# Values of two groups of four heads in one TensorE stretch, a re-planned order, stores held back by a microsecond, and x's low parts on GpSimd

## The chip, the cores and the metric

The kernel runs on one core of a Trainium2 chip. The metric is device time in microseconds (us) of one execution. Three executions of the kernel before took 1021.41, 1022.13 and 1023.31 us; the median is 1022.13.

## The reference

One transformer block on x of 2048 tokens by 640, in fp32: sliding-window attention with 32 heads of 20 (each query sees itself and the 255 keys before it), then a gated feed-forward layer of width 1536, each behind a layer norm and with a residual.

```python
def _A_ref(x, wqkv, wo):
    B, S, D = x.shape
    H = 32; Dh = D // H; W = 256
    qkv = (lambda x, *d: x.transpose(*d))((x @ wqkv).reshape(B, S, 3, H, Dh), 2, 0, 3, 1, 4)
    q, k, v = qkv[0], qkv[1], qkv[2]
    scores = jnp.einsum("bhqd,bhkd->bhqk", q, k) * (Dh ** -0.5)
    idx = jnp.arange(S)
    mask = (idx[:, None] - idx[None, :] >= 0) & (idx[:, None] - idx[None, :] < W)
    scores = jnp.where(mask[None, None], scores, -1e9)
    p = _softmax(scores, axis=-1)
    o = jnp.einsum("bhqk,bhkd->bhqd", p, v)
    return (lambda x, *d: x.transpose(*d))(o, 0, 2, 1, 3).reshape(B, S, D) @ wo

def _B_ref(x, w_gate, w_up, w_down):
    return (_gelu(x @ w_gate) * (x @ w_up)) @ w_down

h = x + _A_ref(_layernorm(x, axis=-1), A_wqkv, A_wo)
h2 = h + _B_ref(_layernorm(h, axis=-1), B_w_gate, B_w_up, B_w_down)
```

## The kernel before

The 2048 tokens are 16 blocks of 128. The dense products (q, k and v, the output projection, the feed-forward layer) split each fp32 operand into a high and a low fp16 part and add three fp16 products. The low part is the operand minus its high part; for x and h of blocks behind the fourth this is done in `turned`: ScalarE writes the high half, VectorE the low half, and two DMA transposes on SP's queue bring both into place (tiles xp, xh, xl).

Attention works block by block in three steps, each on another shape of TensorE's array.

- `maxima` multiplies queries with the keys of the window in tiles of 64 by 64 (rows `ra<-kT,qT` and `rb<-kT,qT`), two heads by two halves of the queries at once. `max_out` lets VectorE add a mask (`mask` for the first two blocks, `band` behind them) and take the row's maximum in one instruction, into `b.mx`; the masked scores themselves go to a bf16 tile `junk` that nobody reads. The maxima are turned and become two extra rows of q.
- `scores` multiplies again, keys as weights, with those extra rows, so that the maximum is subtracted already (`ra<-qT,kT`, `rb<-qT,kT`). `score_out` lets ScalarE take the exponential into an SBUF tile `pt`, and GpSimd clear what lies outside the window with affine selects. A `pt` tile holds four heads (two pairs) and there are three of them; the selects run once for all four heads, when both pairs are there: two of 128x256 and one of 128x512 for a full window.
- `value_lane` multiplies the four heads' `pt` with v, in four column strips of 21 beside each other, fp32 (`pv<-pt,v`). A column of ones in v yields the sum. One stretch is one group of four heads, so a block has eight of them. After every fourth group ScalarE copies the PSUM bank `pv` (oT), and TensorE turns it, VectorE divides, and the result is split for the output projection.

Maxima and scores use the PSUM banks `ra` and `rb` (two banks each), dense products `mm` (two), the values `pv` and transposes `tp`. Between the attention pieces TensorE does dense products: q and k of later chunks of two blocks (weights w0, w1), v (w2), the output projection (w3), and, late, the first feed-forward products. After attention the feed-forward layer runs alone on TensorE.

The order is no list in the source: a planner (`Clock`, `Engine`, and `Lane.start` with the loop behind it) issues the instructions in the order in which it expects them to become ready. `Engine.cost` holds an expected duration for each instruction, `Clock.issue` keeps each engine's expected time, and a lane's next step is issued when the engines that it names are expected to be free soon and its operands to be ready (`self.need() <= now + 0.1`). The steps that only issue a transfer on SP name `("sync",)` alone. SP and ScalarE issue transfers from their queues. While nothing can be issued and no score has been, the planner puts a filler on TensorE: an identity times itself into `pv` (`pv<-ident`).

Rows of the profile carry line 199, the helper through which the planner records every instruction, so tile names tell the steps apart. `PE` rows of fp32 products show two records for one instruction.

## Time and profile before

| | |
|---|---|
| median of three runs | 1022.13 us |
| profiled execution, its own time | 1023.17 us |
| its span, first to last instruction | 1021.3 us |
| TensorE busy | 999.8 us (98%) |
| VectorE busy | 754.8 us (74%) |
| ScalarE busy | 437.0 us (43%) |
| GpSimd busy | 298.0 us (29%) |
| mean granted TensorE clock | 1.00 |

The first values start at 92 us and the last at 574; before lie loads, layer norms and the first projections, behind it the feed-forward layer alone. A group's row reads: line, engine, operation, out<-in by tile names, partitions x elements and type, count, then busy us and mean ns of one, then idle time of the engine just ahead and what ended most of it. A timeline row reads: start, length in us, engine, line, operation, count. PE is TensorE's matmul row, PEld its weight loads, DVE is VectorE, ACT ScalarE, POOL GpSimd, SP SyncE.

### The profile page before, as it was taken

How to read it: one execution, taken by the hardware profiler on the slowest of the kernel's cores; microseconds unless marked ns; L12 is line 12 of the kernel's file. 1: busy time of each engine (PE TensorE's matmuls, PEld its weight loads, DVE VectorE, ACT ScalarE, POOL GpSimd, SP SyncE). 2: the span in 40 equal slices, each digit the busy share in tenths (PEclk: the TensorE clock that was granted, in tenths of full speed). 3: DMA queues.
4: the chain of work that ended last, by engine and by line, in shares of the span. 5: the costliest groups of instructions: out<-in, count | busy, mean ns of one | idle time of the engine just before them, and what ended most of it. 6: DMA issues, size and time to landing. Idle time of an engine off the chain costs nothing.

```text
span 1021.3 us, 30777 instructions
## 1 busy us (share of the span) xinstructions
PE 999.8 (98%) x12921; PEld 695.8 (68%) x12921; DVE 754.8 (74%) x2221; ACT 437.0 (43%) x706; POOL 298.0 (29%) x489
## 2 busy tenths in 40 slices
PE   8999999999999999999999999999999999999998
PEld 7875666676666676776655564567777777777776
DVE  6888998986787787474788788798996975544553
ACT  6514654656555564654558543522222222221220
POOL 7102223443343342342436321255313310000000
PEclk9999999999999999999999999999999999999999
DMA  8657667361551524225033433223553532222211
GB/s 306 137 116 175 184 145 168 81 163 55 91 122 44 114 57 118 42 61 127 3 131 106 92 117 103 78 104 127 161 177 90 161 138 78 78 96 86 78 53 52
DMA packets 105835, 112.67 MB, mean 110 GB/s; under 512 B 38369, under 2 KB 79585, under 8 KB 105697
## 3 DMA queue, kind: packets, MB, share of 16 engines
q1 hardware_dynamic: 93600, 99.97, 35.9%
q10 hardware_dynamic: 12096, 10.75, 3.4%
q8 instruction: 101, 1.65, 0.7%
q14 instruction: 38, 0.30, 0.1%
HBM read 73.73 MB, written 28.84 MB: 100 GB/s over the span
## 4 chain that ended last, share of the span: by engine, by line
PE 82%; DVE 8%; DMA 4%; ACT 2%; issue 2%; SPq 1%; POOL 0%; ACTq 0%; DVEq 0%
PE mm L199 41%; PE pv L199 12%; PE ra L199 11%; PE rb L199 10%; PE tp L199 7%; DVE junk L199 2%; DVE am L199 1%; DVE ht L199 1%; DMA v<-in_wqkv_dram 1%; DMA gu<-in_wqkv_dram 1%; SPq L199 1%; DMA qT<-mT 1%; DVE m L199 1%; ACT pt L199 1%; DMA h_dram<-ht 1%
## 5 line engine op out<-in xcount | busy, mean ns | idle before, releaser
L199 POOL TENSOR_SCALAR_AFFINE_SELECT pt<-pt 128x512 f32<-128x512 f32 x352 | 175.3, 513 | 278.2 <-ACT pt L199 262.6
L199 DVE CUSTOM_DVE_ANT_0 junk<-rb,band 128x320 bf16<-128x320 f32 x230 | 112.5, 489 | 41.3 <-PE rb L199 35.9
L199 DVE CUSTOM_DVE_ANT_0 junk<-ra,band 128x320 bf16<-128x320 f32 x218 | 106.6, 489 | 43.8 <-PE ra L199 38.3
L199 ACT ACTIVATE pt<-ra,esc 128x640 f32<-128x640 f32 (+2 forms) x131 | 99.6, 767 | 66.2 <-PE ra L199 53.3
L199 ACT ACTIVATE pt<-rb,esc 128x640 f32<-128x640 f32 (+2 forms) x125 | 94.9, 766 | 77.2 <-PE rb L199 56.5
L199 PE MATMUL pv<-pt,v 128*21 128x128 f32 x2880 | 104.1, 275 | 1.1 <-ACT oT L199 1.1
L199 PEld LDWEIGHTS <-ah 128*128 128x128 f16 x768 | 75.0, 98 | 29.5 <-issue 2.1
L199 ACT ACTIVATE gel<-gel,ffk 128x512 f32<-128x512 f32 x36 | 26.0, 721 | 138.0 <-DVE gel L199 138.0
L199 PEld LDWEIGHTS pv<-pt,v 128*21 128x21 f32 x2880 | 68.6, 100 | 11.9 <-issue 2.1
L199 PEld LDWEIGHTS <-ws 128*128 128x128 f16 x720 | 70.3, 98 | 8.3
L199 PEld LDWEIGHTS <-kT 62*64 62x64 f16 x2880 | 61.9, 107 | 13.9 <-issue 10.1
L199 PEld LDWEIGHTS <-qT 60*64 60x64 f16 x1280 | 29.8, 104 | 60.3 <-issue 51.3
L199 PEld LDWEIGHTS <-gu 128*128 128x128 f16 x440 | 42.1, 98 | 36.1 <-issue 2.5
L199 DVE SCALAR_TENSOR_TENSOR ht<-mm,ffk,ht 128x320 f32<-128x320 f32 x96 | 52.1, 545 | 10.9 <-PE mm L199 9.0
L199 ACT CAST ah<-gel 128x512 f16<-128x512 f32 x48 | 29.6, 617 | 64.4 <-DVE gel L199 64.2
L199 PE MATMUL mm<-xh,w1h 128*128 128x256 f16 x200 | 54.7, 274 | 1.3 <-DVE qks L199 1.3
L199 PE MATMUL mm<-xl,w1h 128*128 128x256 f16 x200 | 54.7, 273 | 0.0
L199 PE MATMUL mm<-xh,w1l 128*128 128x256 f16 x200 | 54.7, 273 | 0.0
L199 PE MATMUL mm<-w3l,oh 128*128 128x320 f16 x160 | 48.1, 301 | 0.1
L199 PE MATMUL mm<-w2h,xh 128*128 128x320 f16 x160 | 48.1, 300 | 0.0
L199 PE MATMUL mm<-w2h,xl 128*128 128x320 f16 x160 | 48.1, 301 | 0.0
L199 PE MATMUL mm<-w3h,ol 128*128 128x320 f16 x160 | 48.1, 300 | 0.0
(299 smaller groups left out, 2521.3 us busy)
## 6 DMA issues: line engine op xcount, KB each, us to landing
ws<-wsums SPq DMA_DIRECT2D x24, 640.0 KB
qk<-qks ACTq DMA_DIRECT2D x32, 256.0 KB
qT<-qk SPq DMA_DIRECT2D x48, 160.0 KB
kT<-qk SPq DMA_DIRECT2D x48, 160.0 KB
wsums<-ws SPq DMA_DIRECT2D x12, 640.0 KB
ht<-in_x_dram SPq DMA_DIRECT2D x16, 320.0 KB
h_dram<-ht SPq DMA_DIRECT2D x16, 320.0 KB
ht<-h_dram SPq DMA_DIRECT2D x16, 320.0 KB
```

Of the source, the lines that this page charges most:

```text
L199: r = real(*args, **kw)
```

## The change

1. *Values of two groups together.* `pt` tiles now hold one pair of heads, and there are seven (RP) in place of three of two pairs. GpSimd's selects run per pair, at half the width. `value_lane` waits until two groups are ready and multiplies both in one stretch.
2. *VectorE's reduce writes in place.* `junk` goes; the masked scores overwrite their input in PSUM. `mask` and `band` become bf16, and an unused tile of ones goes.
3. *x's low parts by GpSimd.* In `turned`, for x (not for h), the subtraction moves from VectorE to GpSimd.
4. *Expected durations.* `Engine.cost` changes for several operations, and so the order of the whole program does.
5. *Transfers held.* A step that only issues a transfer on SP (but `stack` and `load_lane`) is issued when its operands are expected to have been ready for 1 us (HELD), where before it could be up to 0.1 us ahead of them.

```diff
-            switch, k.mode = SWITCH * (k.mode != mode), mode
+            switch = (SWITCH + 0.02 * (k.mode == "col")) * (k.mode != mode)
+            k.mode = mode
...
             if beside:
-                return 0.004
+                return 0.0005
...
-            return 0.065 + 0.00106 * m + 0.06 * (op == "scalar_tensor_tensor" and len(ins) == 3)
+            extra = {"reciprocal": 0.16, "tensor_tensor_reduce": 0.11}.get(op, 0.0)
+            extra += 0.06 * (op == "scalar_tensor_tensor" and len(ins) == 3)
+            return 0.065 + 0.00106 * m + extra
         if self.name == "scalar":
-            return 0.00084 * n + (0.05 if op == "copy" or len(ins) == 1 else
+            return 0.03 + 0.00084 * n + (0.05 if op == "copy" or len(ins) == 1 else
...
-            return 0.46 if n == 1 else 0.06 + (0.00105 if op == "affine_select" else 0.00203) * n
+            return 0.46 if n == 1 else 0.1 + (0.00105 if op == "affine_select" else 0.00203) * n
...
+    HELD = 1.0
...
-    ones = const.tile([P, P], F32, name="ones")
-    nc.vector.memset(ones, 1.0)
...
         nc.scalar.copy(hi, src)
-        yield on("vector", hi)
-        nc.vector.tensor_tensor(lo, src, hi, op=ALU.subtract)
         if dst:
+            yield on("gpsimd", hi)
+            nc.gpsimd.tensor_tensor(lo, src, hi, op=ALU.subtract)
             to = dst()
+        else:
+            yield on("vector", hi)
+            nc.vector.tensor_tensor(lo, src, hi, op=ALU.subtract)
...
-    mask = wp.tile([P, 2 * P], F32, name="mask")
+    mask = wp.tile([P, 2 * P], BF16, name="mask")
...
-    RV, RK = 5, 6
+    RV, RK, RP = 5, 6, 7
...
-            junk = at("junk", [P, 5 * HB], BF16, 1)
-            nc.vector.tensor_tensor_reduce(junk[:, :w], head,
+            nc.vector.tensor_tensor_reduce(head, head,
...
-        yield on("gpsimd", pt[:, :, 0, :])
...
+        for k in range(pr, pr + pairs(j)):
+            pt = b.pt[k]
+            yield on("gpsimd", pt[:, :, 0, :])
...
+            nc.gpsimd.affine_select(diag, diag, pattern=[[0, 2], [1, P]],
+                                    compare_op=ALU.is_ge, fill=0.0, base=0, channel_multiplier=-1)
+            pos[j, "u", k // 2] += 1
+            if pos[j, "u", k // 2] == 2:
+                valq.append((j, k // 2))
...
-            yield pe(when=lambda: valq and B[valq[0][0]].v == 2 and pos["ones"])
-            j, u = valq.popleft()
+            yield pe(when=lambda: len(valq) > 1 and B[valq[0][0]].v == 2 and pos["ones"])
+            j, u = valq[1]
...
-            yield pe(pt, pv[:, u % 4, :])
...
+            yield pe(*(b.pt[k] for k in range(2 * u - 2, 2 * u + 2)),
+                     pv[:, u % 4 - 1:u % 4 + 1, :])
+            for u in (u - 1, u):
...
+            late = 0.1 if self.engs != ("sync",) or name in ("stack", "load_lane") else -HELD
             return (all(nc.t[e] <= now + back for e in self.engs if e != "sync")
-                    and self.need() <= now + 0.1)
+                    and self.need() <= now + late)
```

Where it moves instructions, first on TensorE in the middle of attention, before: the end of a stretch of scores (weights kT), the values of one group (v of three key blocks, four strips each), then dense products of k.

```order
L199 MATMUL rb<-qT,kT 64x64
L199 LDWEIGHTS kT
L199 MATMUL rb<-qT,kT 64x64
L199 MATMUL pv<-pt,v_122 21x128 x4
L199 MATMUL pv<-pt,v_121 21x128 x4
L199 MATMUL pv<-pt,v_123 21x128 x4
L199 LDWEIGHTS w1h
L199 MATMUL mm<-xh,w1h 128x256
```

And after the change, a like place: scores, one dense product, the values of two groups, and the next maxima.

```order
L199 MATMUL ra<-qT,kT 64x64
L199 LDWEIGHTS xl
L199 MATMUL mm<-w2h,xl 128x320
L199 MATMUL pv<-pt,v_120 21x128 x4
L199 MATMUL pv<-pt,v_119 21x128 x4
L199 MATMUL pv<-pt,v_121 21x128 x4
L199 MATMUL pv<-pt,v_120 21x128 x4
L199 MATMUL pv<-pt,v_119 21x128 x4
L199 MATMUL pv<-pt,v_121 21x128 x4
L199 LDWEIGHTS qT
L199 MATMUL ra<-kT,qT 64x320
```

The same value products stand in half as many stretches, more often between dense products and maxima than between scores and dense products.

On GpSimd in attention, before: the selects of groups of four heads, with a layer norm's root (lyx) among them.

```order
L199 AFFINE_SELECT pt<-pt 128x4x128
L199 AFFINE_SELECT pt<-pt 128x4x64 x2
L199 AFFINE_SELECT pt<-pt 128x4x128
L199 TENSOR_TENSOR lyx<-lvex,mhalf 128x1
L199 AFFINE_SELECT pt<-pt 128x4x64 x2
```

After the change: the selects of pairs, and one of x's subtractions (xp).

```order
L199 AFFINE_SELECT pt<-pt 128x2x64 x2
L199 AFFINE_SELECT pt<-pt 128x2x128
L199 TENSOR_TENSOR xp<-xt,xp 128x640
L199 AFFINE_SELECT pt<-pt 128x2x64 x2
L199 AFFINE_SELECT pt<-pt 128x2x128
```

There are twice as many selects at half the width, and the subtraction stands between one pair's and the next one's.

More of the change, by code (lines that the diff above doesn't have):

```diff
@@ L598, in block_kernel @@
                             compare_op=ALU.is_ge, fill=NEG, base=0, channel_multiplier=1)
-    band = wp.tile([P, 5 * HB], F32, name="band")
+    band = wp.tile([P, 5 * HB], BF16, name="band")
     nc.gpsimd.memset(band, 0.0)
@@ L869, in row_need @@
                                "tensor"))
-        free = 3 - (pos["units"] - pos["values"])
+        free = RP - (pos["parts"] - 2 * pos["values"])
         for j, pr in list(scoreq)[:2]:
             b = B[j]
-            free -= pr % 2 == 0
+            free -= pairs(j)
             if free >= 0:
@@ L952, in scores @@
         b = B[j]
-        u = pr // 2
-        if pr % 2 == 0:
-            b.pt[u] = at("pt", [P, 4, 3, P], F32, 3)
-            pos["units"] += 1
+        for k in range(pairs(j)):
+            b.pt[pr + k] = at("pt", [P, 2, 3, P], F32, RP)
+        pos["parts"] += pairs(j)
         n = len(window(j))
@@ L1010, in score_out @@
-        diag = part(pt, n, n - 1).rearrange("p h a b -> p h (a b)")
-        nc.gpsimd.affine_select(diag, diag, pattern=[[0, 4], [1, P]],
-                                compare_op=ALU.is_ge, fill=0.0, base=0, channel_multiplier=-1)
-        valq.append((j, u))
+        for k in range(pr, pr + pairs(j)):
+            pt = b.pt[k]
+            yield on("gpsimd", pt[:, :, 0, :])
+            if n == 3:
+                half = pt.rearrange("p h a (b c) -> p h (a b) c", b=2)
+                for a, (i, o) in enumerate(((0, 0), (3, 5))):
+                    nc.gpsimd.affine_select(half[:, :, o], half[:, :, i],
+                                            pattern=[[0, 2], [-1, HB]], compare_op=ALU.is_ge,
+                                            fill=0.0, base=-1 - HB * a, channel_multiplier=1)
+            diag = part(pt, n, n - 1).rearrange("p h a b -> p h (a b)")
+            nc.gpsimd.affine_select(diag, diag, pattern=[[0, 2], [1, P]],
[3 more added lines that the diff above has]
+                valq.append((j, k // 2))
@@ L1024, in value_lane @@
             order = [1, 0, 2] if n == 3 else list(range(n))
-            yield pe(pt, pv[:, u % 4, :])
-            for k, i in enumerate(order):
-                for c in range(4):
-                    nc.tensor.matmul(pv[32 * c:32 * c + DH + 1, u % 4, :].rearrange(
-                                         "p (a b) -> p a b", b=HB),
-                                     vring[ks[i] % RV][:, 4 * u + c, :], part(pt, n, i)[:, c],
-                                     start=(k == 0), stop=(k == n - 1))
-            pos["values"] += 1
+            yield pe(*(b.pt[k] for k in range(2 * u - 2, 2 * u + 2)),
+                     pv[:, u % 4 - 1:u % 4 + 1, :])
+            for u in (u - 1, u):
+                valq.popleft()
+                pt = [b.pt.pop(k) for k in (2 * u, 2 * u + 1)]
+                for k, i in enumerate(order):
+                    for c in range(4):
+                        nc.tensor.matmul(pv[32 * c:32 * c + DH + 1, u % 4, :].rearrange(
+                                             "p (a b) -> p a b", b=HB),
+                                         vring[ks[i] % RV][:, 4 * u + c, :],
+                                         part(pt[c // 2], n, i)[:, c % 2],
+                                         start=(k == 0), stop=(k == n - 1))
+                pos["values"] += 1
             if u % 4 == 3:
```

25 lines of the change are left out of this document (6 added, 19 removed).

## The prediction

> **What bounds the kernel now.** First the page's busy times and the chain's shares, then the same engines by stretch of the span (0 to 1021.3 us).
>
> ```profile
> PE 999.8 (98%) x12921; PEld 695.8 (68%) x12921; DVE 754.8 (74%) x2221; ACT 437.0 (43%) x706; POOL 298.0 (29%) x489
> PE 82%; DVE 8%; DMA 4%; ACT 2%; issue 2%; SPq 1%; POOL 0%; ACTq 0%; DVEq 0%
> 0.00:75.00 75.00, 70.50 (x784) 59.79 (x785) 56.99 (x211) 36.42 (x73) 22.34 (x37) 1.00 0.69 190
> 75.00:300.00 225.00, 216.31 (x3832) 149.05 (x3826) 191.93 (x689) 124.67 (x209) 75.39 (x146) 1.00 0.57 133
> 300.00:500.00 200.00, 199.61 (x3854) 139.74 (x3853) 134.62 (x500) 107.34 (x166) 73.36 (x154) 1.00 0.31 74
> 500.00:680.00 180.00, 175.52 (x1941) 101.17 (x1941) 143.90 (x383) 93.62 (x143) 61.33 (x91) 1.00 0.33 104
> 680.00:1021.30 341.30, 337.86 (x2522) 246.03 (x2520) 227.36 (x445) 74.97 (x117) 65.56 (x62) 1.00 0.31 103
> ```
>
> The stretch rows give, behind the length, the busy time of PE, PEld, DVE, ACT and POOL. TensorE is without work for 4.5, 8.7, 0.4, 4.5 and 3.4 us, 21.5 in all, and holds 82% of the chain. The granted clock is 1.00 throughout. So the time is the length of TensorE's own stream plus those holes. VectorE comes next: from 75 to 300 it is busy 191.93 of 225 us, so it has 33 us to spare there, and 65 from 300 to 500.
>
> But "busy" counts a matmul to its modelled end, and neighbours overlap. What a matmul costs the stream is the distance between starts, which the timeline of TensorE shows (start, length, instruction). Four pieces of attention:
>
> ```profile
> 113.13 0.64 PE L199 MATMUL pv<-pt,v 128*21 128x128 f32 x16
> 113.69 0.28 PE L199 MATMUL mm<-xl,w0h 128*128 128x256 f16 x1
> ...
> 300.40 0.31 PE L199 MATMUL ra<-qT,kT 62*64 62x128 f16 x12
> 300.65 0.28 PE L199 MATMUL mm<-xh,w0h 128*128 128x256 f16 x1
> 300.77 0.27 PE L199 MATMUL mm<-xl,w0h 128*128 128x256 f16 x1
> ...
> 301.86 0.27 PE L199 MATMUL mm<-xh,w0l 128*128 128x256 f16 x1
> 302.06 0.33 PE L199 MATMUL rb<-kT,qT 60*64 60x320 f16 x4
> 302.22 0.31 PE L199 MATMUL ra<-qT,kT 62*64 62x128 f16 x12
> 302.46 0.85 PE L199 MATMUL pv<-pt,v 128*21 128x128 f32 x24
> 303.25 0.28 PE L199 MATMUL mm<-xh,w1h 128*128 128x256 f16 x1
> 303.37 0.27 PE L199 MATMUL mm<-xl,w1h 128*128 128x256 f16 x1
> ...
> 410.36 0.30 PE L199 MATMUL mm<-w2h,xh 128*128 128x320 f16 x1
> 410.49 0.30 PE L199 MATMUL mm<-w2l,xh 128*128 128x320 f16 x1
> 410.72 0.85 PE L199 MATMUL pv<-pt,v 128*21 128x128 f32 x24
> 411.50 0.34 PE L199 MATMUL ra<-qT,kT 62*64 62x128 f16 x12
> ```
>
> Dense matmuls of 256 columns start 0.109 us apart (300.77 and, ten later, 301.86). Where the array's shape changes, from 128x128 to the 64-row shape of maxima and scores, the distance is 0.20 (301.86 to 302.06): 0.09 for the change. There are three shapes: dense (128*128), rows (60*64, 62*64), and values (128*21).
>
> **Value stretches: minus 8.3 us.** A value stretch of 24 records takes 0.79 us (302.46 to 303.25). One of 16 records takes 0.56 (113.13 to 113.69), so 8 records are 0.22 and the work of 24 is 0.66. The rest, 0.13, is the change of shape. Going from scores to values (0.24, 302.22 to 302.46) costs what going from scores to dense costs (0.25, 300.40 to 300.65), so a stretch that disappears takes one whole change with it. Where values stand between dense and rows it is the same: 410.49 to 410.72 is 0.23, 0.09 more than the 0.13 between dense matmuls of 320 columns, and 0.78 on to the scores. The change halves the stretches from 128 to 64 with the same 1440 value matmuls: 64 x 0.13 = 8.3.
>
> **Row stretches: minus 4.2 us.** Counted in the two programs' TensorE orders, the unbroken stretches of maxima and scores fall from 264 to 243, with the same 1280 and 2880 matmuls. One between dense matmuls costs 0.09 to enter and about 0.11 to leave (0.25 from the scores' start, of which three steps of 128, 128 and 64 columns are, by the 0.109 of 256, 0.14; and the first dense matmul behind it takes 0.12 for 0.11). 21 x 0.20 = 4.2. Together the changes of shape fall from 657 to 550, and 12.5 us over 107 of them is 0.117 each, near the single ones above.
>
> **Filler: plus 1.8 us.** Until the first score the program puts matmuls of an identity wherever it plans TensorE to wait; these rise from 324 to 388.
>
> ```profile
> 36.94 5.81 PE pv L199 x104
> ```
>
> One takes 5.81 / 104 = 0.056 us, so 64 are 3.6. If they fill waits that VectorE and the loads impose anyway, they cost nothing; if the waits are shorter than planned, they cost all. Both ends are kept, and I take the middle, since 57 of the first 75 us have VectorE busy but not all of them.
>
> **The reduces in place: 0 us on the path.** The masked maxima write onto their own PSUM input instead of into a bf16 tile. No row shows a VectorE instruction that reads and writes one PSUM tile, and bounds come from these.
>
> ```profile
> L199 DVE CUSTOM_DVE_ANT_0 junk<-rb,band 128x320 bf16<-128x320 f32 x230 | 112.5, 489 | 41.3 <-PE rb L199 35.9
> ...
> L199 DVE CUSTOM_DVE_ANT_0 junk<-rb,mask 128x128 bf16<-128x128 f32 x16 | 4.7, 292 | 1.0
> ...
> L199 DVE MEMSET am<- 128x1 f32 x13 | 0.8, 59 | 0.0
> L199 DVE MEMSET pv<- 128x512 f32 x1 | 0.5, 485 | 0.1
> L199 DVE MEMSET ident<- 128x128 f32 x1 | 0.2, 165 | 0.9 <-PEq L1684 0.9
> ```
>
> ```profile
> 75.00:300.00 225.00, 102.93 (x213) 1.00 0.57 133
> 300.00:500.00 200.00, 99.98 (x205) 1.00 0.31 74
> ```
>
> From 128 to 320 columns a reduce grows by 197 ns, 1.03 a column, and 157 are fixed. The worst end is that reading and writing take turns: 320 x 1.03 = 0.33 us more each. The best end is that all of the fixed part were the write's: 0.16 less. The nearest row is the memset: 59 ns for one column and 165 for 128 in SBUF are 0.83 a column, which makes 485 at 512, and the one into PSUM takes 485. A write to PSUM costs VectorE what a write to SBUF costs, so I take 0. The last two rows are the reduces alone by stretch, 213 and 205: VectorE's spare time bears 33 / 213 = 0.155 us more each in the first stretch and 0.32 in the second before TensorE feels it.
>
> [...]
>
> **GpSimd: 0 us on the path.** Each pair of heads gets its own three selects, half as wide, and 12 subtractions of x come over from VectorE.
>
> ```profile
> L199 POOL TENSOR_SCALAR_AFFINE_SELECT pt<-pt 128x256 f32<-128x256 f32 x224 | 89.9, 425 | 246.6 <-ACT pt L199 246.4
> L199 POOL TENSOR_SCALAR_AFFINE_SELECT pt<-pt 128x512 f32<-128x512 f32 x128 | 85.3, 667 | 31.7 <-ACT pt L199 16.3 <-issue 2.7 <-PE ra L199 2.5
> ...
> L199 POOL TENSOR_SCALAR_AFFINE_SELECT mask<-mask 128x128 f32<-128x128 f32 x1 | 0.3, 292 | 0.1
> ...
> L199 POOL TENSOR_TENSOR xl<-gu,xh 128x640 f16<-128x640 f32 x2 | 3.4, 1714 | 0.1
> ```
>
> ```profile
> 302.59 0.79 ACT L199 ACTIVATE pt<-ra,esc 128x640 f32<-128x640 f32 x1
> ...
> 303.45 1.48 POOL L199 TENSOR_SCALAR_AFFINE_SELECT pt<-pt 128x256 f32<-128x256 f32 x3 [1.89 <-ACT pt L199]
> ```
>
> ```profile
> L199 POOL TENSOR_SCALAR_AFFINE_SELECT pt<-pt x352: 409/415/1185, 91.3 to 573.1; 128x256 f32<-128x256 f32 x112, 128x512 f32<-128x512 f32 x64
> ...
> L199 DVE TENSOR_TENSOR xp<-xt,xp x12: 814/820/1261, 44.5 to 371.3; 128x640 f16<-128x640 f32 x12
> ```
>
> For four heads: 2 x 425 + 667 = 1.52 us before, 2 x (2 x 292 + 425) = 2.02 after, so 128 groups cost GpSimd 64 us more, and the subtractions 12 x 1.7 = 21. It is idle for 247 + 32 us in front of these selects alone. The last two rows are all selects and, on VectorE, the subtractions (shortest, median, longest in ns). VectorE gives up 12 x 0.82 = 10 us, none of it TensorE's. Behind a subtraction in GpSimd's queue stand selects, and behind those a value stretch: each can come 1.7 us late, if it finds no slack. The slack: the scores that start at 302.22 have their exponential at 302.59, which takes 0.79, and the selects follow at 303.45. With 1.01 for three narrow ones that is 2.24 us from the scores' start to the values, some 2.3 with the last hand-over. In the new order the TensorE work from the start of the last scores to their value stretch is worth 2.8 us in the median, at the distances above (4.1 before, with longer selects). It fits narrowly, so I take 0 and keep a rival for it.
>
> **Holes: minus 2 us.** The first row is from the waits of SP's queue (in total, times, longest), the second a piece of the chain:
>
> ```profile
> SPq L199 <- DVE ht L199: 219.1, 29, 40.8
> ```
>
> ```profile
> 227.78 5.63 DMA h_dram<-ht
> ```
>
> SP's queue stood 219 us for rows of h that VectorE was still adding to, 41 at the longest, and the loads behind stood with it; one store is in the chain. Placing a store 1 us later in the order lets loads go ahead of it. It can also be late for whoever reads h next, which is a stage away. The holes of 75 to 680 are 13.6 us; new places of everything can close or add a good part of them. I take 2 off, with 7 either way. The dropped ones tile and bf16 masks move nothing on TensorE.
>
> **The sum.** 1021.3 - 8.3 - 4.2 + 1.8 - 2 = 1008.6 for the span. The profiled execution took 1023.17, 1.9 more than its span: 1010.5. The median of the runs, 1022.13, is 1.0 below that execution, so about 1009.5; I say 1010.
>
> **Rivals.** *The plan also closes holes:* if durations nearer the chip's remove two thirds of the 13.6 us, that is 7 more, and the filler costs nothing: 1001. For it: the old order has such holes at all. Against: the longer ones hang on DMAs. 15%.
>
> *VectorE keeps the pace from 75 to 300:* it is 85% busy there, and 213 of the 512 reduces lie in it, 0.42 of attention. What TensorE saves there would come back as holes, 0.42 x 12.5 = 5.2, and with the whole filler, 1.8 more, 1017. Against: VectorE's work there is the same or less, and dense work can be drawn forward. 12%.
>
> *Values wait for GpSimd:* with 0.5 us between 2.3 and 2.8, a select that is held late shows on TensorE at once. The longest select lasted 1185 ns, where the wide ones lasted 667 in the mean. A mean wait of 0.1 us over 64 stretches is 6.4: 1016. For it: more and shorter selects share the engine with long subtractions. Against: idle time of 279 us. 10%. [...]
>
> *The other side, reduces in place take turns in PSUM:* 0.33 us more on each. From 75 to 300 that is 213 x 0.33 = 70 us against 33 spare: 37 longer, and 3 more up to 500: 1010 + 40 = 1050. It decides from 0.155 us a reduce on. Only the memset row speaks against it. 7%.
>
> *The change does not do what it says:* the order already shows 64 value stretches of double length, so only their price is open; if a change hid behind weight loads and cost half, the sum is 1016. It is within the row distances' reach, so 4%.
>
> **How the numbers follow.** The forecast, 52%, is 1010 with 1005 to 1015. The range goes from 1001, the first rival, to 1019, past the three milder ones; the turn-taking case stays outside. A measurement of this kernel tells about 0.2%, 2 us. Faster, below 1020.1: 52 + 15 + 12, with 5 of the 10 for values that wait and 3 of the 4 for the half price, 87%. Within 0.2%: 3 more of those 10, where the waits are longer than priced, and the last of the 4, 4%. Slower: the other 2 of the 10 and the 7, 9%.
>
> **What would show it.** Value stretches of 48 records taking about 1.45 us (2 x 0.66 + 0.13). The reduce, now ra<-ra or rb<-rb, at 489 ns. TensorE idle from 75 to 680 near 12 us and no waits of value matmuls on POOL. If the reduce takes over 0.65 us, or value stretches wait for selects, the prediction is wrong.

## The result, and the profile after

The changed kernel takes **1039.51 us** (median of 4 runs, 1037.67 to 1040.06) where the kernel before, beside it on the same chip, takes 1021.77 (1020.8 to 1023.31): 1.0172 times as long, 95% interval 1.0154 to 1.0190. The prediction was 1010, so it was wrong in sign and by 29.5 us. The profiled execution's span is 1038.3 us, 17.0 more than before. Three executions of those below lie far outside the others of their kernel (1129.7 us in e3, 3427.8 in e7, 1967.3 of the kernel before beside e13 to e16); the medians count them, the ratios do not.

First the page of the changed kernel: busy times, and the chain's shares.

```profile
PE 1002.0 (97%) x12985; PEld 715.5 (69%) x12985; DVE 761.8 (73%) x2208; ACT 435.8 (42%) x706; POOL 375.7 (36%) x853
PE 83%; DVE 9%; ACT 3%; DMA 2%; issue 1%; POOL 0%; SPq 0%; ACTq 0%; POOLq 0%; DVEq 0%
```

TensorE still holds the chain, but it is busy 2.2 us more, although it changes shape 107 times less, and without work for 36.3 us where it was 21.5. The stretches of the changed kernel, in the same columns as in the prediction (length, then PE, PEld, DVE, ACT, POOL, then the granted clock):

```profile
0.00:75.00 75.00, 71.00 (x786) 61.05 (x787) 55.49 (x196) 36.20 (x72) 24.43 (x39) 1.00 0.66 188
75.00:300.00 225.00, 217.28 (x3697) 158.95 (x3696) 186.30 (x656) 118.95 (x204) 101.81 (x263) 0.99 0.54 133
300.00:500.00 200.00, 191.53 (x3808) 138.87 (x3806) 142.38 (x499) 105.47 (x162) 100.05 (x310) 0.97 0.32 72
500.00:680.00 180.00, 175.31 (x2121) 104.08 (x2120) 137.80 (x391) 92.96 (x142) 74.25 (x172) 0.98 0.31 92
680.00:1038.30 358.30, 346.87 (x2577) 252.57 (x2577) 239.83 (x469) 82.25 (x128) 75.15 (x70) 0.99 0.33 105
```

The stretch from 300 to 500 stands out: 0.4 us without work before, 8.5 now, at a clock of 0.97. The loss lies between 438 and 510 us, a stretch of many short waits that is called the hole from here on. The timeline of TensorE inside it, with the idle time ahead of a row and what ended it in brackets:

```profile
469.18 0.34 PE L199 MATMUL rb<-kT,qT 60*64 60x128 f16 x8
469.35 0.32 PE L199 MATMUL ra<-qT,kT 62*64 62x128 f16 x12
470.77 0.34 PE L199 MATMUL rb<-kT,qT 60*64 60x128 f16 x8 [1.11 <-DVE mxs L199]
470.94 0.32 PE L199 MATMUL ra<-qT,kT 62*64 62x128 f16 x12
472.21 0.33 PE L199 MATMUL ra<-kT,qT 60*64 60x128 f16 x8 [0.96 <-ACT pt L199]
472.36 0.42 PE L199 MATMUL rb<-qT,kT 62*64 62x128 f16 x12
473.73 0.48 PE L199 MATMUL rb<-kT,qT 60*64 60x128 f16 x8 [0.95 <-ACT pt L199]
473.95 0.53 PE L199 MATMUL ra<-qT,kT 62*64 62x128 f16 x12
474.40 2.77 PE L199 MATMUL pv<-pt,v 128*21 128x128 f32 x48
```

Maxima and scores follow each other with nothing between them. Each pair of rows takes half a microsecond and then waits 0.95 to 1.11 us for the bank, which the exponential or the reduce still holds. In the prediction's pieces from 300 us, dense products lie between scores and maxima. Here there are none. The dense matmuls alone (`mm`), from 430 to 520 us, in the kernel before and then in the changed one (length, busy, count, clock):

```profile
430.00:520.00 90.00, 51.28 (x340) 1.00 0.29 77
```

```profile
430.00:520.00 90.00, 32.55 (x186) 0.89 0.33 78
```

340 dense matmuls lay in this stretch, now 186. The missing ones were done earlier, as one weight of k shows (count, shortest, median and longest ns, first and last start), before and then after:

```profile
L199 PE MATMUL mm<-xl,w1h x200: 270/273/284, 26.1 to 466.8; 128*128 128x256 f16 x100
```

```profile
L199 PE MATMUL mm<-xl,w1h x200: 270/273/417, 25.8 to 419.7; 128*128 128x256 f16 x100
```

The products of k end at 420 us instead of 467. And the granted clock goes down in the hole, to 0.89 in the mean of the 90 us shown above. Pieces of the changed kernel's chain between 430 and 520 us (start, length, work):

```profile
436.37 1.44 PE pv L199 x48
...
442.91 2.60 PE pv L199 x48
...
466.62 2.64 PE pv L199 x48
...
474.48 2.70 PE pv L199 x48
```

Stretches of the same kernel with all engines, in the columns used above: the first of these value stretches, the waits ahead of the second, and then the second to the fourth.

```profile
436.30:437.80 1.50, 1.50 (x60) 1.29 (x56) 1.27 (x5) 0.79 (x1) 0.21 (x1) 1.00 0.13 37
438.00:442.80 4.80, 1.92 (x80) 1.47 (x68) 3.35 (x13) 2.39 (x3) 3.27 (x12) 0.89 0.38 118
442.84:445.50 2.66, 2.66 (x60) 2.05 (x57) 1.07 (x4) 0.79 (x1) 1.30 (x4) 0.56 0.02 6
466.55:469.20 2.65, 2.65 (x53) 1.99 (x52) 0.83 (x4) 0.89 (x2) 1.06 (x4) 0.53 0.07 22
474.40:477.20 2.80, 2.80 (x61) 2.03 (x58) 1.08 (x4) 0.79 (x1) 1.31 (x4) 0.50 0.67 119
```

The same 48 value matmuls take 1.44 us at a granted clock of 1.00, and 2.60, 2.64 and 2.70 us at 0.56, 0.53 and 0.50. The lower clock comes with short waits: none is longer than 1.11 us from 430 to 520 us, but from 438.0 to 442.8 us TensorE is busy for 1.92 of 4.80 us, at a clock of 0.89, and the value stretch right behind runs at 0.56.

A second loss stands at the start of the feed-forward layer, and one wait makes it:

```profile
PE tp L199 <- DVE ws L199: 8.4, 1, 8.4
```

### The profile page after: what moved, and what is told of

Its sections match the earlier page's. It is cut to its first block, busy times and chain, and to the rows that moved or that the text cites. A ratio compares the mean times of both kernels' runs of the same rounds, so it can differ in the third digit from the quotient of the medians.

```text
span 1038.3 us, 31355 instructions
## 1 busy us (share of the span) xinstructions
PE 1002.0 (97%) x12985; PEld 715.5 (69%) x12985; DVE 761.8 (73%) x2208; ACT 435.8 (42%) x706; POOL 375.7 (36%) x853
## 4 chain that ended last, share of the span: by engine, by line
PE 83%; DVE 9%; ACT 3%; DMA 2%; issue 1%; POOL 0%; SPq 0%; ACTq 0%; POOLq 0%; DVEq 0%
PE mm L199 40%; PE pv L199 14%; PE ra L199 12%; PE rb L199 10%; PE tp L199 7%; DVE rb L199 2%; DVE ra L199 1%; ACT pt L199 1%; DVE am L199 1%; DVE mxs L199 1%; DVE qks L199 1%; DMA wst<-in_wd_dram 1%; ACT wst L199 1%; DMA wst<-in_wg_dram 0%; DVE ht L199 0%
## 5 line engine op out<-in xcount | busy, mean ns | idle before, releaser
L199 POOL TENSOR_SCALAR_AFFINE_SELECT pt<-pt 128x128 f32<-128x128 f32 (+1 forms) x704 | 238.3, 356 | 232.0 <-ACT pt L199 214.4
L199 DVE CUSTOM_DVE_ANT_0 rb<-rb,band 128x320 f32<-128x320 f32 x236 | 117.5, 498 | 38.6 <-PE ra L199 17.7
L199 DVE CUSTOM_DVE_ANT_0 ra<-ra,band 128x320 f32<-128x320 f32 x212 | 105.4, 497 | 51.5 <-PE rb L199 35.4
L199 PE MATMUL pv<-pt,v 128*21 128x128 f32 x2880 | 96.9, 283 | 0.0
L199 PEld LDWEIGHTS pv<-pt,v 128*21 128x21 f32 x2880 | 76.6, 104 | 13.4 <-issue 8.3
L199 PEld LDWEIGHTS <-kT 62*64 62x64 f16 x2880 | 65.7, 108 | 10.1 <-issue 6.6
L199 DVE DVE_READ_ACCUMULATOR2_ANT mxs<- 128x1 f32 x512 | 72.2, 141 | 0.0
L199 POOL TENSOR_TENSOR gelt<-gelt 128x256 f32<-128x256 f32 x18 | 15.9, 883 | 114.9 <-ACT gelt L199 114.9
L199 POOL TENSOR_TENSOR rr<-rr 128x256 f32<-128x256 f32 x18 | 14.3, 796 | 105.5 <-ACT rr L199 105.5
L199 PE MATMUL rb<-kT,qT 60*64 60x320 f16 (+4 forms) x668 | 42.6, 287 | 7.8 <-ACT pt L199 5.4
```

Of the source, the lines that this page charges most:

```text
L199: r = real(*args, **kw)
```

## The experiments

Each is given with its median, and with its ratio to runs of the kernel before on the same chip and that ratio's 95% interval. The groups of experiments ran on different chips, on which the kernel before took 1020.95 to 1023.68 us, so medians from different groups can be compared to some 2 us. Two quantities are used throughout. *Work left for blocks 10 to 12* is an estimate: TensorE's matmuls between the first values of block 10 and those of block 13 in a program's order, at the distances of the prediction. It is 80 us before (18, 44, 18) and 68 after (24, 20, 24). *Planned distance* is what the planner expects from one reduce to the next. It follows from the source: a reduce of 320 columns costs 0.065 + 0.00106 x 320 = 0.404, and these lines add 0.18 where the output is a tile of a ring of one, as `junk` is:

```python
    LAT = 0.18
...
                lat = self.LAT if e != eng else (0.1 if e in ("vector", "gpsimd") else 0.0)
...
        if len(ring) == bufs:
            self.wr[key] = [((0, 128, 0, 1 << 30), "ring", self.quiet(ring[0]))]
```

The tile's last use is noted as another engine's write. So before, the planner spaced two reduces by 0.584 us, and left VectorE free in 0.18 of it. The change took `junk` out and added 0.11: 0.514, all of it busy.

### Which part: durations, pairing, in place (e1 to e4)

e1_old_durations undoes all edits of `Engine.cost` in the changed kernel:

```diff
-            extra = {"reciprocal": 0.16, "tensor_tensor_reduce": 0.11}.get(op, 0.0)
-            extra += 0.06 * (op == "scalar_tensor_tensor" and len(ins) == 3)
-            return 0.065 + 0.00106 * m + extra
+            return 0.065 + 0.00106 * m + 0.06 * (op == "scalar_tensor_tensor" and len(ins) == 3)
...
```

> The changed kernel with the planner's expected durations as they were before, all else as changed. By the order theory (the raised durations, above all 0.11 us on the masked reduce, make the plan pull dense products ahead of attention until they run out near block 10) the holes of 18 us from 430 to 525 and of 8.5 us at 679 shrink to a few us, value stretches stay 64 long ones, and the time is 1005 to 1015. By the in-place theory (VectorE's reduce with its accumulator read takes 67 ns longer, 34 us in all, and TensorE waits for it whatever the order) it stays above 1030.

1035.35 us, 1.0119 (1.0084 to 1.0154): still slow, but otherwise. The long holes are gone, and blocks 10 to 12 keep 82 us of work. Many short waits have come, of which these lead from 50 to 600 us (us in total, times, longest):

```profile
PE rb L199 <- DVE mxs L199: 5.0, 13, 0.9
PE ra L199 <- DMA kT<-qk: 3.9, 3, 2.4
PE ra L199 <- DVE mxs L199: 3.5, 11, 0.6
```

e2_reduce_duration undoes only the 0.11:

```diff
-            extra = {"reciprocal": 0.16, "tensor_tensor_reduce": 0.11}.get(op, 0.0)
+            extra = {"reciprocal": 0.16}.get(op, 0.0)
```

> The changed kernel without one number, the 0.11 us that the plan adds to the masked reduce. Order theory: this one number spaces attention out; time 1005 to 1020, holes from 430 to 525 below 6 us. In-place theory: above 1030. If both this and the run with all old durations stay slow, the order theory falls.

1037.80 us, 1.0151 (1.0117 to 1.0184). Both came out above 1030, where the theory of the dearer in-place reduce had put them, so the durations seemed cleared. In both kernels the planned distance is 0.404, a number that becomes important below.

e3_single_groups is the changed kernel with value stretches of one group:

```diff
-            yield pe(when=lambda: len(valq) > 1 and B[valq[0][0]].v == 2 and pos["ones"])
-            j, u = valq[1]
+            yield pe(when=lambda: valq and B[valq[0][0]].v == 2 and pos["ones"])
+            j, u = valq[0]
...
```

> The changed kernel with value stretches of one group again (about 120 in place of 64), durations and all else as changed. Theory that pairing itself holds attention back (four pairs of heads must be ready, the pt tiles are taken): faster than the changed kernel, 1025 or less. Order theory: about 80 more changes of shape at 0.117 us are 9 us more, but an order of its own with less starved blocks; between 1030 and 1050.

1025.71 us, 1.0027 (1.0003 to 1.0052): 14 us faster than with pairs, although it changes shape 80 times more. That pointed at pairing itself.

e4_in_place_same_order keeps the order of before and only lets the chip write the reduce over its input; the planner is not told:

```diff
-            r = real(*args, **kw)
+            r = real(args[1], *args[1:], **kw) if op == "tensor_tensor_reduce" else real(*args, **kw)
```

> The kernel before in its own order, instruction for instruction, where the masked reduce alone writes onto its PSUM input in place of the bf16 tile. It shows the price of the in-place write by itself: reduce 498 and accumulator read 141 ns as in the changed kernel, 34 us more on VectorE. In-place theory: 1035 or more, since VectorE has only 33 us to spare from 75 to 300. Order theory: 1022 to 1030.

1026.48 us, 1.0031 (1.0013 to 1.0049): 4.7 us more than the kernel before beside it (1021.79), in the same order; by the ratio's interval it is 1.3 to 5.0.

### Pairing alone (e5 to e8)

e5_pairs_alone undoes everything but the pairing, with a bf16 tile for the reduces and six parts for seven:

```diff
...
-    RV, RK, RP = 5, 6, 7
+    RV, RK, RP = 5, 6, 6
...
-            nc.vector.tensor_tensor_reduce(head, head,
+            junk = at("junk", [P, 5 * HB], BF16, 1)
+            nc.vector.tensor_tensor_reduce(junk[:, :w], head,
...
-    HELD = 1.0
+    HELD = -0.1
...
-            nc.gpsimd.tensor_tensor(lo, src, hi, op=ALU.subtract)
+            nc.vector.tensor_tensor(lo, src, hi, op=ALU.subtract)
```

> The changed kernel with everything undone but the pairing of value groups (with its parts of two heads per pair, here six of them, and narrow selects): reduces write into their own bf16 tile, the planner's durations are the old ones, stores are not held, x's low parts stay on VectorE. 576 changes of shape against 657 before and 550 after, and the planned order keeps dense work in every block. Theory A (waiting for two groups slows attention's own cycle, whatever else is done): holes eat the 10 us of shape changes and more, 1025 to 1035. Theory B (the pairing is sound, and it is the dearer in-place reduce that makes VectorE pace attention once the pairs have taken TensorE's changes away): 1011 to 1015, since 81 changes at 0.117 are 9.5 less and nothing else costs.

**1013.91 us**, 0.9918 (0.9889 to 0.9946). Theory A fell: with pairs alone the kernel gains 8.3 us, where the 81 changes of shape are worth 9.5. It beats both kernels. Its stretches from 75 to 680:

```profile
75.00:300.00 225.00, 221.19 (x3864) 158.25 (x3865) 189.56 (x680) 125.08 (x211) 99.65 (x278) 1.00 0.57 135
300.00:500.00 200.00, 196.66 (x3898) 140.64 (x3899) 140.20 (x522) 109.07 (x168) 100.75 (x318) 0.98 0.34 85
500.00:680.00 180.00, 177.57 (x1943) 105.41 (x1941) 144.50 (x381) 94.78 (x144) 76.82 (x152) 1.00 0.30 93
```

TensorE is without work for 9.6 us there, 4.0 less than before, and waits for a select only here:

```profile
PE pv L199 <- POOL pt L199: 0.8, 2, 0.5
```

e6_after_own_tile is the changed kernel's order (but for two changes of shape) with a tile for the reduces that the planner doesn't know:

```diff
+            if op == "tensor_tensor_reduce":
+                r = real(OWN[0][:, :args[0].free_size()], *args[1:], **kw)
...
```

> The changed kernel with six parts for seven (the order stays the same but for two changes of shape) and its reduces written into a bf16 tile of their own, without telling the planner: the same order, only the 67 ns and the longer write are gone. If the in-place price only adds (4.7 us in the order of before), 1034 to 1036. If it is what makes VectorE the pace of attention in this order (Theory B), 1015 to 1025. The hole between 438 and 510 us, with no dense product in it, should stay under theory A.

1035.29 us, 1.0114 (1.0083 to 1.0145), 4.2 us below the changed kernel. So the in-place write is not what makes this order slow, and neither is the seventh part.

e7_pairs_in_place is e5's order with e4's edit:

```diff
-            r = real(*args, **kw)
+            r = real(args[1], *args[1:], **kw) if op == "tensor_tensor_reduce" else real(*args, **kw)
```

> The kernel of e5_pairs_alone, same order, with the reduces written in place: only the in-place price, now under paired values. Additive: 4 to 6 us above e5_pairs_alone. Theory B: 10 to 20 us above it, because VectorE, 0.13 us slower per pair of heads, holds the row banks that long.

1019.82 us, 0.9975 (0.9956 to 0.9994): 5.9 above e5_pairs_alone. Theory B fell too.

e8_single_own_tile is the changed kernel without pairs, in-place reduces and new durations; two-head parts, held stores and GpSimd's x stay:

```diff
-            yield pe(when=lambda: len(valq) > 1 and B[valq[0][0]].v == 2 and pos["ones"])
+            yield pe(when=lambda: valq and B[valq[0][0]].v == 2 and pos["ones"])
...
-            nc.vector.tensor_tensor_reduce(head, head,
+            nc.vector.tensor_tensor_reduce(junk[:, :w], head,
...
-            extra = {"reciprocal": 0.16, "tensor_tensor_reduce": 0.11}.get(op, 0.0)
...
```

> What is left of the change without pairing, without in-place reduces and with the old durations: two-head parts, narrow selects, held stores, x's low parts on GpSimd. 643 changes of shape against 657, 334 fillers against 324. Both theories: 1018 to 1023. If held stores or GpSimd's longer queue cost something by themselves, above 1025.

1023.34 us, 1.0012 (0.9993 to 1.0031), 0.3 above the range expected and below the 1025 that would have spoken against held stores or GpSimd's longer queue.

### What is added to the pairs (e9 to e12)

On e5_pairs_alone, e9_pairs_held puts the held stores back:

```diff
-    HELD = -0.1
+    HELD = 1.0
```

> The kernel of e5_pairs_alone (1013.9) with stores held a microsecond more in the order, and nothing else. If holding stores costs when values are paired (theory H: loads or later reads of h come late), 1020 or more; if not, 1012 to 1017.

1021.84 us, 0.9998 (0.9982 to 1.0014), as theory H expected. e10_pairs_x_low puts GpSimd's subtraction back:

```diff
-            nc.vector.tensor_tensor(lo, src, hi, op=ALU.subtract)
+            nc.gpsimd.tensor_tensor(lo, src, hi, op=ALU.subtract)
```

> The kernel of e5_pairs_alone with x's low parts by GpSimd and nothing else: 12 subtractions of some 1.4 us stand in GpSimd's queue between selects. If paired values wait for them (theory G), 1020 or more with value matmuls waiting on GpSimd's selects; if not, 1012 to 1017.

1020.62 us, 0.9991 (0.9969 to 1.0014): the time that theory G expected, but without its sign, since no value matmul waits for a select. e11_pairs_held_x_low puts both back:

```diff
-    HELD = -0.1
+    HELD = 1.0
...
-            nc.vector.tensor_tensor(lo, src, hi, op=ALU.subtract)
+            nc.gpsimd.tensor_tensor(lo, src, hi, op=ALU.subtract)
```

> Both on top of e5_pairs_alone: what is left of the changed kernel beside this are the new durations and the in-place reduces. If neither of the two costs (theory D: the durations bring the loss), 1012 to 1018; if they cost together, 1025 or more, as in e1_old_durations, which has them, the pairs, old durations and in-place reduces and took 1035.

1015.02 us, 0.9936 (0.9913 to 0.9959). Either edit alone seems to cost 7 us, both together 1. So these are not prices that add up, and they are read here as how far a new order scatters; that the two edits make up for each other is not ruled out. e9's loss, for one, has the wait at the feed-forward layer in it,

```profile
PE tp L199 <- DVE ws L199: 6.4, 1, 6.4
```

which e5 has for 0.8 us. By that reading, a difference below some 8 us between two orders says nothing of an edit, and the 8.3 us of e5 stand at this border. e12_new_durations_pairs takes both out of the changed kernel, so that pairs, in-place reduces and the new durations stay:

```diff
-    HELD = 1.0
+    HELD = -0.1
...
-            nc.gpsimd.tensor_tensor(lo, src, hi, op=ALU.subtract)
+            nc.vector.tensor_tensor(lo, src, hi, op=ALU.subtract)
```

> The changed kernel without held stores and with x's low parts on VectorE: pairs, new durations, in-place reduces. Its order leaves as little dense work beside blocks 10 to 12 of attention as the changed kernel's. Theory D: 1033 to 1040, with the hole between 430 and 520 us. Theories H and G: about 1019 to 1024, pairs and in-place reduces alone being 1019.8.

1039.08 us, 1.0168 (1.0140 to 1.0195), with 69 us of work for blocks 10 to 12 and the same hole. The loss comes with the durations: e7, with pairs and in-place reduces but the old durations, takes 1019.8.

### One planned number (e13 to e18)

e13_one_duration is e11 with one number more in the planner, which makes the planned distance 0.404 + 0.18 + 0.11 = 0.694. The chip's instructions are the same but for 94 fillers more at the start; their order is not:

```diff
-            return 0.065 + 0.00106 * m + 0.06 * (op == "scalar_tensor_tensor" and len(ins) == 3)
+            extra = {"tensor_tensor_reduce": 0.11}.get(op, 0.0)
+            extra += 0.06 * (op == "scalar_tensor_tensor" and len(ins) == 3)
+            return 0.065 + 0.00106 * m + extra
```

> The kernel of e11_pairs_held_x_low (1015.0) with one number more: the planner's reduce is 0.11 us longer. The planner keeps a fresh tile 0.18 behind its last use, so back to back it now plans a reduce every 0.69 us, where the chip takes 0.489 and 0.083. Its order has 428 fillers (334 there: 94 x 0.056 = 5 us) and leaves 21, 24 and 19 us of TensorE's work for blocks 10 to 12 of attention, where that kernel has 28 each. Theory R (the dense work runs out beside those blocks, and TensorE waits there, then runs with its clock down): 1030 to 1038, with the hole at 430 to 520 us, though not one instruction of the chip has changed its price. Rival (the loss was the in-place reduce in an order that thinks it short): 1013 to 1020.

**1050.88 us**, 1.0268 (1.0238 to 1.0299): 36 us above e11 (34 by the two ratios), more than theory R expected. The first values come 25 us later, and the hole is there. TensorE is without work for 39.7 us of the span after 20.3 in e11, and 17.8 of these 19.4 us lie between 300 and 520 us. Its own work is 17.9 us longer: the mean clock, 0.984 after 0.997, is an estimated 13.6 us of 1048.8, and the fillers 5 by the expectation. Dense matmuls from 430 to 520 us in e11, and then in e13:

```profile
430.00:520.00 90.00, 52.65 (x306) 1.00 0.31 85
```

```profile
430.00:520.00 90.00, 32.15 (x199) 0.93 0.40 95
```

TensorE's longest waits of that stretch in e13; e11 has none:

```profile
PE ra L199 <- ACT pt L199: 6.9, 7, 1.3
PE rb L199 <- ACT pt L199: 5.8, 6, 1.0
```

e14_fill_waits is the changed kernel with fillers in the hole:

```diff
+            elif (64 <= pos["values"] < 112 and nc.t["tensor"] <= now and opened["mm"] < banks["mm"]
+                  and nc.slot(psums["mm"], "mm", banks["mm"]) <= now):
+                t = bank("mm")
+                nc.tensor.matmul(t[:, :P], ident16, ident16, start=True, stop=True)
+                done("mm")
```

> The changed kernel, and where its planner finds TensorE waiting in blocks 8 to 13 it puts matmuls of the identity into a free bank of the dense products, some 200 of them, 11 us of work that nobody reads and 25 more changes of shape. If half of that hole is the clock that goes down when TensorE waits (a value stretch takes 2.6 us there instead of 1.44), more work makes the kernel faster: 1026 to 1034. If the hole is the wait alone, 1039 to 1044.

1038.20 us, 1.0146 (1.0120 to 1.0171), between the two expectations and not to be told from the changed kernel. All engines from 430 to 520 us in the changed kernel, and then in e14:

```profile
430.00:520.00 90.00, 78.76 (x1656) 55.86 (x1644) 60.83 (x214) 44.58 (x67) 43.68 (x139) 0.89 0.33 78
```

```profile
430.00:520.00 90.00, 89.55 (x1778) 61.29 (x1774) 61.35 (x214) 44.35 (x67) 42.84 (x136) 0.98 0.29 76
```

TensorE is now busy all the time at a clock of 0.98, one value stretch is slow (2.29 us in the timeline) instead of four (2.62 to 2.77 there, where most have 1.51), and blocks 10 to 12 take 94 us instead of 93. So filling the waits kept the clock up and did not shorten the hole, and the lower clock looks like a consequence of the waits. It is not shown to be only that: the clock's 0.09 over 90 us are 8 us, and the fillers' own work, 11 us by the expectation, lies in the same balance and may have held attention up by as much.

e15_in_place_old_plan is e11's order with e4's edit, so that all of the change is there but the durations and the seventh part:

```diff
-            r = real(*args, **kw)
+            r = real(args[1], *args[1:], **kw) if op == "tensor_tensor_reduce" else real(*args, **kw)
```

> The kernel of e11_pairs_held_x_low, same order, its reduces written in place on the chip while the planner still plans a tile of their own: everything that the change does, except the durations (and six parts for seven). In-place adds its 4 to 6 us: 1019 to 1021. If in-place, held stores and GpSimd's x cost together, as e1_old_durations at 1035 may be read, 1030 or more.

**1015.66 us**, 0.9920 (0.9889 to 0.9951), below the 1019 to 1021 expected. In-place costs 0.6 us here or nothing; it cost 4 to 6 in three other orders.

e16_reduce_by_0_18 is e1 with a planned reduce 0.18 us longer, 0.584, all of it busy:

```diff
+                    + 0.18 * (op == "tensor_tensor_reduce"))
```

> e1_old_durations (1035.3, small waits everywhere) with one number more: the planner's reduce 0.18 us longer, so that back to back it plans 0.58 as it did with a tile of its own. Its order leaves 23, 20 and 23 us for blocks 10 to 12. Theory R: the small waits before 100 us shrink and the hole at 430 to 520 us comes: 1028 to 1036. If only the planned distance of the two reduces mattered: 1019 to 1023.

1043.09 us, 1.0193 (1.0149 to 1.0237), 7 us beyond what theory R expected, with 66 us for blocks 10 to 12 and the hole. The same distance as before, but counted as VectorE's work, makes the order slow.

e17_old_durations_six is e1 with six parts; from e15 it differs only in that the planner, too, sees the reduces in place:

```diff
-    RV, RK, RP = 5, 6, 7
+    RV, RK, RP = 5, 6, 6
```

> e1_old_durations with six parts for seven, as in e15_in_place_old_plan; beside that kernel (1015.7) the only difference left is that the planner, too, sees the reduces in place, and so no longer keeps the 0.18 us between two of them: it plans 0.40 from one to the next where the chip takes 0.498 and 0.141. If that is what e1_old_durations lost its time to: 1030 to 1037, with waits of the row banks on reduces spread over attention. If it was the seventh part: 1014 to 1020.

1040.13 us, 1.0186 (1.0161 to 1.0211), 24 us above e15 and 3 beyond the range expected. Its waits on reduces from 50 to 600 us; e15 shows none among its longest:

```profile
PE rb L199 <- DVE mxs L199: 5.9, 16, 0.9
...
PE ra L199 <- DVE mxs L199: 4.4, 14, 0.6
```

e18_pairs_true_act is e5 with ScalarE's 0.03 us alone:

```diff
-            return 0.00084 * n + (0.05 if op == "copy" or len(ins) == 1 else
+            return 0.03 + 0.00084 * n + (0.05 if op == "copy" or len(ins) == 1 else
```

> The kernel of e5_pairs_alone with one of the new durations, ScalarE's 0.03 us more (the exponential planned at 0.71, 0.79 on the chip). 566 changes of shape, 28, 28 and 26 us left for blocks 10 to 12. Theory R: fast like its siblings, 1010 to 1018, since the dense work does not run out; if any of the new durations spoils the order, 1025 or more.

1016.75 us, 0.9954 (0.9932 to 0.9975): fast like its siblings.

All together, with pairs unless said otherwise (planned distance of two reduces, with b where all of it counts as busy; the chip's, from the reduce and its accumulator read; work left for blocks 10 to 12; time that the chip takes for them, from first values to first values; us throughout):

| kernel | planned | chip | work left | time taken | median |
|---|---|---|---|---|---|
| before, single groups | 0.584 | 0.572 | 80 | 85 | 1021.8 |
| e3, single groups | 0.514 b | 0.64 | 84 | 89 | 1025.7 |
| e5 | 0.584 | 0.572 | 78 | 88 | 1013.9 |
| e11 | 0.584 | 0.572 | 84 | 88 | 1015.0 |
| e15 | 0.584 | 0.64 | 84 | 89 | 1015.7 |
| e1 | 0.404 b | 0.64 | 82 | 89 | 1035.4 |
| e17 | 0.404 b | 0.64 | 78 | 84 | 1040.1 |
| after | 0.514 b | 0.64 | 68 | 93 | 1039.5 |
| e12 | 0.514 b | 0.64 | 69 | 98 | 1039.1 |
| e16 | 0.584 b | 0.64 | 66 | 97 | 1043.1 |
| e13 | 0.694 | 0.572 | 64 | 91 | 1050.9 |

Two failures can be told apart. Planned far too short (0.404 for 0.64), the reduce is late all along, and rows of attention stand in TensorE's queue before their bank is free. The waits on reduces are 10.3 us in e17, where TensorE is without work for 36.2 us in the whole span and for 22.0 in e15; the rest of the 24 us between the two is not assigned. e2, with 0.404 too, is not in the table: its blocks 10 to 12 take 98 us, of which TensorE is without work for 2.7. Planned as more of VectorE's time, attention looks slower to the planner than the chip runs it. It draws dense work forward to fill the waits that it sees, and blocks 10 to 12 have too little left: with 78 to 84 us of work they take 84 to 89, and with 64 to 69 they still take 91 to 98. TensorE is without work for 11.2, 13.2, 16.1 and 14.5 us of them in the changed kernel, e12, e16 and e13, and for at most 3.2 us in the seven kernels above these in the table; of the rest of the gap, the lower clock is an estimated 10, 12, 8 and 6 us (in the same order 0.89, 0.87, 0.91 and 0.93 from 430 to 520 us, a stretch of 90, where e5 has 0.96, and the kernel before, e1, e11 and e15 have 1.00), and the 4 to 7 us that remain are as in the seven, with 4 to 10. This is shown for the planned number (e11 and e13, e15 and e12, where e12's other differences cost little by e7 and e6); that the planner sees attention as slower is read from its source and from the earlier end of k's products (420 us for 467 above; 433 in e13 for 442 in e11, though e13's attention starts 25 us later).

## Why the prediction was wrong, step by step

**Value stretches, minus 8.3: right.** There are 64 stretches, and the 56 that have 48 records take 1.44 us at a granted clock of 1.00, 1.45 foretold. (The starts shown in the prediction give 0.23 for 8 records, where it says 0.22; the trace's nanoseconds, 785 and 569, bear the 0.22 out.)

**Row stretches, minus 4.2: agrees, but was not measured by itself.** The changes of shape are a count from the orders, and e5, with 81 fewer and three fillers more, gains 8.3 us where 0.117 each gives 9.5 less 0.2. e9, with as many, gains 0.4, so the times alone do not settle it. TensorE's busy time, which leaves waits out, says more: it is 991.3 to 994.5 us in e5, e9, e10, e11 and e18, 5.3 to 8.5 below the 999.8 of before, although their clocks of 0.993 to 0.998 add an estimated 2 to 7 us.

**Filler, plus 1.8: not settled by itself.** From 0 to 75 us TensorE is without work for 4.0 us after 4.5. The first values start at 101.6 instead of 92.2, but e3 starts as late and loses little.

**In place, 0 on the path: mis-sized, and the row was a wrong neighbour.** The reduces and their accumulator reads, before (the read alone; the reduces stand in the prediction) and then after:

```profile
L199 DVE DVE_READ_ACCUMULATOR2_ANT mxs<- 128x1 f32 x512 | 42.3, 83 | 0.0
```

```profile
L199 DVE CUSTOM_DVE_ANT_0 rb<-rb,band 128x320 f32<-128x320 f32 x236 | 117.5, 498 | 38.6 <-PE ra L199 17.7 <-PE rb L199 15.8 <-ACT h0h L199 0.6
...
L199 DVE CUSTOM_DVE_ANT_0 ra<-ra,band 128x320 f32<-128x320 f32 x212 | 105.4, 497 | 51.5 <-PE rb L199 35.4 <-PE ra L199 12.1
...
L199 DVE DVE_READ_ACCUMULATOR2_ANT mxs<- 128x1 f32 x512 | 72.2, 141 | 0.0
```

The reduce itself takes 9 ns more, the read of its accumulator right behind it 58: 67 together, 34 us of VectorE over 512. A memset that only writes (485 ns for 512 columns into PSUM, in the kernel before) showed nothing of that. That the write itself pays it is not shown, as 58 of the 67 ns are the read's. The price lies inside the bounds (of which the fixed part, 157 ns, should read 161: 489 less 320 x 1.026), and below the 0.155 us a reduce up to which VectorE's spare time was to bear all of it. Yet the path pays 4.7, 5.9, 4.2 and 0.6 us for it, each good to 2 to 4 by the intervals (e4, e7 and e15 in fixed orders, e6 but for two changes of shape).

**GpSimd, 0: right.** Value matmuls don't wait for it in the changed kernel, 0.8 us in e5, and e11 with x's low parts there takes 1015.0.

**Holes, minus 2 with 7 either way: this is the step that failed.** From 75 to 680 us TensorE is without work for 20.9 us, not 12, and in the whole span for 14.8 more than before; and its own work, foretold 10.7 shorter, is 2.2 longer. The sum had no term for the clock: it took over the 1.00 of the kernel before, and the mean is now 0.985, where 1.5% of 1038.3 is 15.6 us. 16.8 of holes and 12.9 of work are the 29.7 by which the span misses the 1008.6 of the sum. The step priced the durations as new places that close or add holes at random, scaled by the holes that were there. But a duration in the planner also says how fast attention can go, and so how much dense work is drawn ahead. e11 and e13, which differ in that one number, differ by 36 us. Of the 14.8 us, 7.3 lie from 75 to 680, where this shows; most of the rest is the wait for `ws` at the start of the feed-forward layer, whose cause is open. The store queue, on which the step looked instead, did get shorter,

```profile
SPq L199 <- DVE ht L199: 173.8, 26, 29.3
```

from 219.1 us, and it brought nothing.

None of the rivals was this one. *The plan also closes holes* had the right place and the wrong sign: it took durations nearer the chip's for a better order. *VectorE keeps the pace from 75 to 300* is off: it is busy 186.3 of 225 us. *Turn-taking* would have shown a reduce of 0.8 us.

Open are three things. Why single groups with the same 0.514 keep their dense work (28, 29 and 27 us in e3): pairing and durations act together, and how was not tried. What decides the wait of the feed-forward layer for `ws`, 8.4 us in the changed kernel, 6.4 in e9, 0.8 in e5. And how far the clock by itself lengthens the hole, for which e14 leaves room up to some 8 us.

## What to carry to other kernels

A planner's durations are not only a matter of truth: with a fixed supply of filling work, they set how early it is spent, so count in the new order how much is left in each stage, above all in the last ones, before pricing a re-plan as noise. Durations and dependences that look idle (the tile that nobody read, with its 0.18 us) may be what keeps the order right; take one out only with a look at what the planner makes of it. And before an edit's price is read from two re-planned kernels, hold the order and change the chip's instruction alone: orders here lay up to 8 us apart without a reason that was found, and the price of the in-place reduce was under 6.

## What the runs showed of the hardware

A reduce of 320 columns that writes over its PSUM input took 498 ns in the changed kernel, where one that writes a bf16 tile took 489 in the kernel before; the accumulator's read behind it took 141 ns instead of 83. And TensorE's granted clock was 0.89 from 430 to 520 us in the changed kernel, though no wait there was longer than 1.11 us: from 438.0 to 442.8 us TensorE was busy for 1.92 of 4.80 us, and the 48 value matmuls right behind took 2.60 us at a clock of 0.56, instead of 1.44 at 1.00. With identity matmuls in the waits (e14) the clock was 0.98 from 430 to 520 us.
